# Attention, FFN and gate in one kernel: every third VectorE exp pair as four shifted fp16 terms, made by GpSimd integer adds

## The chip, the cores and the metric

The kernel runs on one core of a Trainium2 chip. A core has TensorE (PE: matmuls, with its weight loads shown as PEld), VectorE (DVE), ScalarE (ACT), GpSimd (POOL) and SyncE (SP, which here only issues DMAs). They run side by side, each through its own queue in order, and wait for each other through semaphores. The metric is the time of one execution on the device in microseconds, where smaller is better. All times here are in microseconds unless marked ns.

## What is computed

A layer norm of `x` (2048 tokens, 512 wide) feeds two branches: attention with 32 query heads of 16 that share one key head and one value head, and a gated FFN of width 1792. The FFN branch, through a silu, gates the attention branch:

```python
xn = layernorm(x)
q = (xn @ wq) as 32 heads of 16;  k = xn @ wk;  v = xn @ wv
p = softmax(q @ k.T * 16 ** -0.5)
s = concat_heads(p @ v) @ wo
g = silu((silu(xn @ w_gate) * (xn @ w_up)) @ w_down)
out = x + s * g
```

The softmax needs 32 x 2048 x 2048 exponentials, 134 million. They are the bulk of the elementwise work.

## The kernel before

**Tiling.** The attention is cut into 32 blocks (`NBLK`): 4 groups of 512 queries, 4 groups of 8 heads, and 2 halves of 4 heads. In a block, each of 16 key tiles of 128 gives two score tiles (`x` is 0 or 1) of 128 keys by 2 heads by 512 queries, 1024 columns of PSUM; 1024 score tiles in all. A score tile is two matmuls (`sc_emit`, line 856) into one of three PSUM slots, `ring[0]` to `ring[2]`. The matmuls p times v of a block accumulate in the PSUM tile `o_ps`; the ones columns in the value weights (`VA`, `VD`) yield the softmax denominator beside it. All scores are scaled so that one unit of exponent of two is 1024.

**Two ways to the exponential.** A tile in `ring[0]` or `ring[1]` goes to ACT (`act_sc`, line 914): one exp of 128x1024 into a buffer `Pb` in bf16 (the first eight tiles of block 1 go into free space, `XB`). Two such tiles give one group of four PE matmuls with the weights `VA`.

A tile in `ring[2]` goes to DVE (`dve_sc`, line 934), two tiles to a pair. "Pass A" (line 942) adds a bias to the score and writes it as uint16 into `Ub`. Read as fp16, those bits are a piecewise linear approximation of two to the power of the score. For the pair's 2048 columns, `dM` (line 955) keeps the mantissa bits and sets an exponent, giving a number between 0.5 and 1; `dE` (line 958) keeps the exponent bits; `dW` (line 960) multiplies the mantissa number by the original. The two results, `Eb` and `Wb`, enter `o_ps` as two terms, weighted by `CE` and `CW` in the two copies of `VD`: a constant plus a quadratic in the mantissa, so that the sum follows the exponential. Each term is one group of four PE matmuls. There are three `Ub` and two each of `Eb` and `Wb`.

**FFN and projections.** Their matmuls are "fill" groups through one PSUM tile, `m_ps`, spread between the score tiles (`g_ffn`, `g_down`, `g_q`, `g_out`). ACT takes a tanh of each, DVE the products. At the end of each pair of blocks the denominators go by DMA through `dn`, a reciprocal, the DRAM scratch `dscr` and a broadcast into `rb`; GpSimd then multiplies `oa` by `rb` into `oT` (line 711). `g_out` multiplies by `wo`, DVE by the gate, and GpSimd adds `x`, which stays in SBUF in `x_sb` (line 675). SP stores the rows.

**What sets the order.** A planner in the kernel, `_Sched`, runs while the program is built. Every operation has an engine, an assumed duration (an ACT exp 0.904, pass A and `dW` 1.135, `dM` and `dE` 0.6, a PE group 0.215), dependencies and a priority. `pe_pick` decides at each step whether PE issues a score tile for ACT, a score tile for DVE, or a ready group; DVE picks pass A before `dM`, `dE` and `dW`. The planned order is then fixed on each engine by `chain`, so each engine's queue runs in exactly that order. When an operation comes later than planned, all that stands behind it on the engine waits. In the prologue `x` is normalised and transposed, 4 rows of 128 tokens at a time; the last four rows of the output have a tail of their own.

Of the kernel before, what the change touches and what calls it, by code (L numbers as in the profile page):

```python
# [1 line left out]

# [8 lines left out]
FP16 = mybir.dt.float16  # L11
# [14 lines left out]
COFF = 4.0  # L26
CE, CW = 0.66858732, 0.66372796 * 1.0
DEN_LO = 16.0
# [5 lines left out]
PB_URG, AHEAD, LAZY, ACTMIN, ACTLOW = 6, 16, 8, 1.7, 1.5  # L34
TOL, MERGE = 0.12, 0.1

# [145 lines left out]
class _Sched:  # L182
    LAT = {"PE": 0.205, "ACT": 0.22, "DVE": 0.25, "POOL": 0.16, "DMA": 0.0, "EXT": 0.0}
    SAME = {"PE": 0.0, "ACT": 0.0, "DVE": 0.1, "POOL": 0.05, "DMA": 0.0}
    SWITCH = 0.105
    HOT = 0.3

    def __init__(self):
        self.free = {"PE": 0.0, "ACT": 0.0, "DVE": 0.0, "POOL": 0.0, "DMA": 0.0}
        self.ready = {e: [] for e in self.free}  # L190
        self.done = []
        self.pe_log = []
        self.seq = 0
        self.mode = None
        self.key = lambda o: o.prio
# [31 lines left out]
    def switch(self, mode):  # L227
        return self.SWITCH if self.mode is not None and mode != self.mode else 0.0

    def pick(self, e):  # L230
        lst = self.ready[e]
        if not lst:
            return None
        if e == "DMA":
            op = min(lst, key=lambda o: (o.ready, o.seq))
            return op.ready, op
        t = self.free[e]
        tm = max(t, min(o.ready for o in lst))
        now = [o for o in lst if o.ready <= tm + 1e-9]
        best = min(now, key=lambda o: (self.key(o), o.seq))  # L240
        if e == "DVE":
            hot = [o for o in lst if o.ready > tm and self.key(o)[0] < 1.6 and self.key(o) < self.key(best)]
            if hot:
                h = min(hot, key=lambda o: (o.ready, o.seq))
                fit = [o for o in now if tm + o.dur <= h.ready + self.HOT]
                best = min(fit, key=lambda o: (self.key(o), o.seq)) if fit else h
        return max(t, best.ready), best

    def place(self, op, start):
        e = op.eng  # L250
        op.start = start
        if e == "PE":
            op.start += self.switch(op.mode)
            self.mode = op.mode
        op.end = op.start + op.dur
        if e != "DMA":
            self.free[e] = op.end
        self.done.append(op)
        if e == "PE":
            self.pe_log.append(op)  # L260
        for u in op.users:
            u.left -= 1
            if u.left == 0:
                self._arm(u)
# [7 lines left out]
def kernel(  # L272
# [79 lines left out]
    vf = sb([P, NT, DH], FP32, "vf")  # L352
    VD = sb([P, 2, NT, 3 * DH], FP16, "VD")
    stats = sb([P, NT, nc.vector.BN_STATS_DIM], FP32, "stats")
    mv = sb([P, NT, nc.vector.BN_AGGR_DIM], FP32, "mv")
# [4 lines left out]
    QB = [sb([P, 512], BF16, f"QB{i}") for i in range(2)]  # L360
    NPB, NU, NE = 8, 3, 2
    Pb = [sb([P, 1024], BF16, f"Pb{i}") for i in range(NPB)]
    XB = [g2_sb[:, 2 * i:2 * i + 2, :].rearrange("p n d -> p (n d)") for i in range(NT // 2)]
    Ub = [sb([P, 2048], U16, f"Ub{i}") for i in range(NU)]
    Eb = [sb([P, 2048], U16, f"Eb{i}") for i in range(NE)]
    Wb = [sb([P, 2048], U16, f"Wb{i}") for i in range(NE)]
    th = [sb([P, 512], FP32, f"th{i}") for i in range(1)] * 2
# [120 lines left out]
    MMF = 0.215  # L488
    NBLK = NSC * NQ * 2
    NTILE = NBLK * NT * 2  # L490
    NPAIR = NSC * NQ
# [14 lines left out]
    def pro_x(c, pr, banks, ev_eng):  # L506
# [3 lines left out]
        for n0 in range(4 * c, 4 * c + 4, step):  # L510
# [22 lines left out]
            for n in range(n0, n0 + step):  # L533
                xo = OP("DVE", 0.33, [r, xr_rel[n % 4]], lambda n=n: e_xn(n), (pr - 0.15 if c == 0 else pr - 0.05, n),
                        name="xn")
                bk = banks[n % 4 // pk]
                h = n % pk
                t_ = OP("PE", 0.26, [xo, brel[bk]] + grp, lambda n=n, bk=bk, h=h: e_tr(n, bank[bk], h), (pr, n), "f",
                        "tr")
                xr_rel[n % 4] = t_  # L540
                grp = grp + [t_]
                if len(grp) == pk:
                    ee = ev_eng if n not in (1, 3) else "DVE"
                    ev = OP(ee, 0.5 if ee == "ACT" else 0.34 if pk == 1 else 0.6, grp,
                            lambda n=n, bk=bk, ee=ee: e_txe(n + 1 - pk, pk, bank[bk], ee), (pr - 0.1, n), name="txe")
                    if c:
                        held.append((grp[0], ev, bk))
                    grp = []
                    brel[bk] = ev
                    evs.append(ev)  # L550
# [24 lines left out]

    held = []
    evs = pro_x(0, 0.3, ("0a", "0b", "1a", "1b"), "ACT")
# [20 lines left out]
    for c in range(1, NSC):  # L598
# [7 lines left out]
        pro_v(c, evs, "2a", 0.7 + 0.01 * c)  # L606
    d_gate = [brel["2a"], brel["2b"], brel["m"]]

    m_rel = [brel["m"]]
# [63 lines left out]
    def e_out_add(n, src, eng):  # L673
        r = res[n % 4]
        return eng.tensor_tensor(out=r[:, :D], in0=src[:, :D], in1=x_sb[:, n, :], op=ALU.add)

# [3 lines left out]
    def g_out(n):  # L680
# [6 lines left out]
        m_rel[0] = m_  # L687
        ad = OP("POOL", 1.3, [m_, xr_rel[n % 4]], lambda: e_out_add(n, ab[i], nc.gpsimd), (0,), name="oadd")
        ab_rel[i] = ad
# [75 lines left out]
    unp = [[[], []] for _ in range(NBLK)]  # L765
    cur = {"ba": 0, "lastx": 1, "nA": 0, "exp": None, "pair": None, "np": 0, "issued": 0, "lastsc": None, "junk": 0, "nX": 0}
    slot = [None, None, None]
    pb_rel, w_rel, e_rel, wop_rel = [], [], [], []
    open_block(0)
# [126 lines left out]

    def act_sc(i, b, x, start):
        sc, t = place_sc(i, b, x, start, MMF)
        cur["lastx"] = x
# [11 lines left out]
        if k >= NPB:  # L911
# [3 lines left out]
                (1,), name="exp")  # L915
        cur["exp"] = ex
        slot[i] = ex
        unp[b][x].append((ex, k, t, buf))
# [16 lines left out]

    def dve_sc(b, x, start, dur):
        sc, t = place_sc(2, b, x, start, dur)
        first = cur["pair"] is None
        u = cur["np"]
        ui = u % NU  # L940
        pa = OP("DVE", 1.135, [sc, wop_rel[u - NU] if u >= NU else None],
                lambda: nc.vector.tensor_scalar(out=Ub[ui][:, x * 1024:(x + 1) * 1024], in0=ring[2][:], scalar1=ubias,  # L942
                                                scalar2=UINF, op0=ALU.add, op1=ALU.min), (1.5, u), name="passA")
        slot[2] = pa
        if first:
            cur["pair"] = (b, x, t, pa)
            return
        _, x0, t0, pa0 = cur["pair"]
        cur["pair"] = None
        cur["np"] += 1  # L950
        pair_blk.append(b)
        half = b % 2
        tx = {x0: t0, x: t}
        ei = u % NE
        o1 = OP("DVE", 0.6, [pa, pa0, w_rel[u - NE] if u >= NE else None], lambda: nc.vector.tensor_scalar(  # L955
            out=Wb[ei][:], in0=Ub[ui][:], scalar1=0x3FF, scalar2=0x3800, op0=ALU.bitwise_and,
            op1=ALU.bitwise_or), (2, u, 0), name="dM")
        o2 = OP("DVE", 0.6, [pa, pa0, e_rel[u - NE] if u >= NE else None], lambda: nc.vector.tensor_scalar(  # L958
            out=Eb[ei][:], in0=Ub[ui][:], scalar1=0x7C00, scalar2=None, op0=ALU.bitwise_and), (2, u, 1), name="dE")
        o3 = OP("DVE", 1.135, [o1, o2], lambda: nc.vector.tensor_tensor(  # L960
            out=Wb[ei][:].bitcast(FP16), in0=Wb[ei][:].bitcast(FP16), in1=Ub[ui][:].bitcast(FP16), op=ALU.mult),
            (2, u, 2), name="dW")
        wop_rel.append(o3)
        for i, (buf, o, rel) in enumerate(((Eb[ei], o2, e_rel), (Wb[ei], o3, w_rel))):
            mms = []
            dps = [o, oev[b - 1]]
            for g in range(4):
                tt = tx[g // 2]
                mms += mm_of(VD[:, i], lambda g, buf=buf: buf[:].bitcast(FP16)[:, g * 512:(g + 1) * 512], tt, half, (g,))
                dps.append(v_ready[tt // 4][i + 1])  # L970
            pv = OP("PE", MMF, dps, pv_emit(b, mms), (1, b, cur["nA"]), "c", "dpv")
            rel.append(pv)
            blk_pv[b].append(pv)
        check_done(b)
# [10 lines left out]
    LB = NBLK - 1  # L985
    LN = 4 * (NSC - 1)

# [99 lines left out]
    def pe_pick():  # L1087
# [42 lines left out]
        if tm is not None:  # L1130
            if ts is None or tm + sd.switch(co.mode) + co.dur <= ts + TOL:
                cands.append(tm)
            else:
                tm = None
        if td is not None and (ts is None or td + sd.switch("r") + MMF <= ts):
            if tm is None or td < tm - 0.2:
# [31 lines left out]
    def pe_do(start, what):  # L1168
# [20 lines left out]
        if kind == "dve":  # L1189
            dve_sc(arg[0], arg[1], start, MMF)  # L1190
            return
# [16 lines left out]
        if dt is not None and tile_ready(*dt) is not None:  # L1208
            at = max(sd.free["PE"], sd.avail(slot[2], "PE"), tile_ready(*dt))
            dve_sc(dt[0], dt[1], at, 0.015 if dt[1] != x else MMF)  # L1210

# [118 lines left out]
```

## Time and profile before

| what | value |
|---|---|
| median of 4 executions (lowest, highest) | 785.98 (784.04, 793.15) |
| the profiled execution | 790.09 |
| its span on the core | 788.3 |
| mean granted PE clock of the span | 0.986 |
| exps on ACT, into `Pb` and into the free space | 770 + 8 |
| pairs on DVE: pass A; `dM`, `dE`, `dW` | 246; 123 each |
| groups on POOL: `oT`; the adds of `x` (both forms) | 15; 14 |
| chain that ended last, by engine | PE 34%, ACT 33%, DVE 20%, issue 9% |

In the profile a group is all instructions of one line, operation and shape. Its busy time is the time in which at least one of them ran; its mean is the length of one. On ACT neighbouring instructions overlap, so that the mean (1167 ns for an exp) is longer than the distance from one to the next. A wait names the instruction that ended it. The chain is followed back from the last instruction to what released each step.

### The profile page before, as it was taken

To read this page: it belongs to the slowest core of one execution; us is meant where nothing else is said; L and a number is where in the kernel's file an instruction comes from. 1 tells how busy PE (TensorE), PEld (TensorE's weight loads), DVE (VectorE), ACT (ScalarE), POOL (GpSimd) and SP (SyncE) were. 2 spreads that over 40 slices of the span, in tenths; PEclk is the share of its full clock that TensorE was granted. 3 is DMA by queue.
4 is the path that set the end of the run, shared out by engine and by line. 5 is a ranking of instruction groups with operands and counts; after the bars stand their busy time and mean duration, and the time that the engine had idled before them with its cause. 6 is when DMAs were issued, how large, how long until landed. Compare 5 with 4: busy or idle time off the path is not lost.

```text
span 788.3 us, 19520 instructions
## 1 busy us (share of the span) xinstructions
PE 726.4 (92%) x8097; PEld 218.8 (28%) x8098; DVE 739.3 (94%) x925; ACT 757.4 (96%) x864; POOL 48.0 (6%) x59
## 2 busy tenths in 40 slices
PE   7999899999999999999989999989999989999994
PEld 3332222222232222222222222222222222222221
DVE  7678999999999999999999989999999989999997
ACT  6899999999999999999999989999999989999993
POOL 2100000000011000001001000000001100000001
PEclk9999999999999999999999889999999989999998
DMA  9300000000010000000000000000001000000001
GB/s 329 114 3 7 17 3 22 2 10 15 5 35 15 23 3 9 16 1 23 3 22 22 16 15 3 22 3 9 16 2 35 16 22 3 3 21 2 23 2 32
DMA packets 19464, 18.50 MB, mean 23 GB/s; under 512 B 8552, under 2 KB 15464, under 8 KB 19368
## 3 DMA queue, kind: packets, MB, share of 16 engines
q1 hardware_dynamic: 17496, 16.37, 6.8%
q8 instruction: 65, 1.06, 0.6%
q10 hardware_dynamic: 1872, 0.82, 0.4%
q14 instruction: 31, 0.25, 0.1%
HBM read 12.62 MB, written 2.34 MB: 19 GB/s over the span
## 4 chain that ended last, share of the span: by engine, by line
PE 34%; ACT 33%; DVE 20%; issue 9%; DMA 1%; SPq 1%; POOL 0%; ACTq 0%; DVEq 0%
ACT Pb L914 28%; PE ring L856 14%; PE m_ps L474 12%; PE o_ps L726 7%; DVE Ub L942 7%; DVE Wb L960 4%; ACT th L637 3%; DVE Eb L958 2%; DVE Wb L955 2%; ACT th L654 1%; SPq L753 1%; DMA dn<-oa 1%; DVE ab L639 1%; DVE hT L643 1%; DVE oa L739 1%
## 5 line engine op out<-in xcount | busy, mean ns | idle before, releaser
L914 ACT ACTIVATE Pb<-ring 128x1024 bf16<-128x1024 f32 x770 | 728.7, 1167 | 11.2 <-PE ring L856 10.9
L856 PE MATMUL ring<-QB,KT 32*128 32x512 bf16 x2048 | 320.8, 383 | 40.9 <-ACT Pb L914 32.8
L942 DVE TENSOR_SCALAR Ub<-ring 128x1024 uint16<-128x1024 f32 x246 | 299.3, 1216 | 13.4 <-PE ring L856 8.5
L856 PEld LDWEIGHTS <-KT 32*128 32x128 bf16 x2048 | 106.1, 91 | 350.1 <-issue 345.6
L960 DVE TENSOR_TENSOR Wb<-Wb,Ub 128x2048 f16<-128x2048 f16 x123 | 150.4, 1223 | 0.0
L726 PE MATMUL o_ps<-Pb,VA 128*32 128x512 bf16 x1540 | 149.7, 389 | 0.4 <-DVE oa L739 0.4
L955 DVE TENSOR_SCALAR Wb<-Ub 128x2048 uint16<-128x2048 uint16 x123 | 86.9, 708 | 0.1
L958 DVE TENSOR_SCALAR Eb<-Ub 128x2048 uint16<-128x2048 uint16 x123 | 86.1, 705 | 0.0
L474 PE MATMUL m_ps<-xnT,wg_sb 128*32 128x512 bf16 x896 | 74.0, 384 | 0.5 <-DVE g_sb L656 0.3
L474 PE MATMUL m_ps<-xnT,wu_sb 128*32 128x512 bf16 x896 | 71.6, 392 | 1.3 <-DVE ab L639 1.2
L474 PE MATMUL m_ps<-wd_sb,hT 128*32 128x512 bf16 x896 | 71.9, 383 | 0.0
L711 POOL TENSOR_TENSOR oT<-oa,rb 128x512 bf16<-128x512 f32 x15 | 20.7, 1379 | 608.8 <-DMA rb<-dscr 560.8
L726 PEld LDWEIGHTS <-VA 128*32 128x32 bf16 x1556 | 38.7, 94 | 54.8 <-issue 54.1
L726 PE MATMUL o_ps<-Eb,VD 128*32 128x512 f16 x492 | 48.7, 390 | 2.1 <-DVE Eb L958 1.8
L726 PE MATMUL o_ps<-Wb,VD 128*32 128x512 f16 x492 | 49.1, 389 | 1.4 <-DVE Wb L960 0.9
L637 ACT ACTIVATE th<-m_ps 128x512 f32<-128x512 f32 x56 | 41.9, 749 | 0.0
L726 PEld LDWEIGHTS <-VD 128*32 128x32 f16 x984 | 29.4, 94 | 43.1 <-issue 41.0
L643 DVE TENSOR_TENSOR hT<-ab,m_ps 128x512 bf16<-128x512 f32 x56 | 38.1, 680 | 2.7 <-PE m_ps L474 2.4
L639 DVE SCALAR_TENSOR_TENSOR ab<-th,m_ps 128x512 f32<-128x512 f32 x56 | 38.0, 678 | 1.6 <-ACT th L637 1.0
L474 PEld LDWEIGHTS <-wg_sb 128*32 128x32 bf16 x896 | 17.3, 94 | 27.3 <-issue 26.5
L474 PEld LDWEIGHTS <-wu_sb 128*32 128x32 bf16 x896 | 16.6, 95 | 27.1 <-issue 24.9
L739 DVE COPY oa<-o_ps 128x512 f32<-128x512 f32 (+1 forms) x33 | 22.0, 668 | 1.5 <-PE o_ps L726 1.5
(106 smaller groups left out, 246.2 us busy)
## 6 DMA issues: line engine op xcount, KB each, us to landing
rb<-dscr SPq DMA_DIRECT2D x15, 256.0 KB
dn<-oa SPq DMA_DIRECT2D x120, 2.0 KB, 1.7
oa<-oa SPq DMA_DIRECT2D x60, 32.0 KB, 2.0
wg_sb<-in_B_w_gate_dram SPq DMA_DIRECT2D x1, 1792.0 KB, 12.0
wu_sb<-in_B_w_up_dram SPq DMA_DIRECT2D x1, 1792.0 KB
wd_sb<-in_B_w_down_dram SPq DMA_DIRECT2D x1, 1792.0 KB, 19.8
out_dram<-xn SPq DMA_DIRECT2D x14, 128.0 KB, 2.0
x_sb<-in_A_x_dram SPq DMA_DIRECT2D x3, 512.0 KB
```

The costliest lines, as they stand in the source:

```text
L474: return [nc.tensor.matmul(out=dst[GRP * j:GRP * j + GRP, :], lhsT=w[:, GRP * j:GRP * j + GRP], rhs=rhs, start=start, stop=stop, tile_posi ...
L637: t_ = OP("ACT", 0.477, [a], lambda: nc.scalar.activation(out=th[i][:], in_=m_ps[:], func=ACT.Tanh, scale=0.5), (0,), name="tanh")
L639: s_ = OP("DVE", 0.6, [t_, ab_rel[i]], lambda: nc.vector.scalar_tensor_tensor(out=ab[i][:], in0=th[i][:], scalar=1.0, in1=m_ps[:], op0=ALU ...
L643: h = OP("DVE", 0.6, [b], lambda: nc.vector.tensor_tensor(out=hT[:, f, :], in0=ab[i][:], in1=m_ps[:], op=ALU.mult), (1,), name="hmul")
L726: r.append(nc.tensor.matmul(out=o_ps[GRP * g:GRP * g + GRP, :], lhsT=lhs, rhs=rhs, start=(n == 0), stop=(n == pv_total[(b, g)] - 1), tile_ ...
L739: oev[b] = sd.new(_Op("DVE", 0.6, [], lambda: [nc.vector.tensor_copy(out=oat[:, a:z], in_=o_ps[:, a:z]) for a, z in cuts], (0.2,), name="o ...
L856: return lambda: [nc.tensor.matmul(out=ring[sl][:, u * 512:(u + 1) * 512], lhsT=KT[half][GRP * g:GRP * g + GRP, t * P:(t + 1) * P], rhs=QB ...
L914: lambda: nc.scalar.activation(out=buf, in_=ring[i][:], func=ACT.Exp, scale=escale, bias=ebias),
L942: lambda: nc.vector.tensor_scalar(out=Ub[ui][:, x * 1024:(x + 1) * 1024], in0=ring[2][:], scalar1=ubias, scalar2=UINF, op0=ALU.add, op1=AL ...
L955: o1 = OP("DVE", 0.6, [pa, pa0, w_rel[u - NE] if u >= NE else None], lambda: nc.vector.tensor_scalar(out=Wb[ei][:], in0=Ub[ui][:], scalar1 ...
L958: o2 = OP("DVE", 0.6, [pa, pa0, e_rel[u - NE] if u >= NE else None], lambda: nc.vector.tensor_scalar(out=Eb[ei][:], in0=Ub[ui][:], scalar1 ...
L960: o3 = OP("DVE", 1.135, [o1, o2], lambda: nc.vector.tensor_tensor(out=Wb[ei][:].bitcast(FP16), in0=Wb[ei][:].bitcast(FP16), in1=Ub[ui][:]. ...
```

## The change

`dve_sc` gets a second form. Where the pair's number is a multiple of `KE` = 3, GpSimd's planned backlog is under `KB` = 3 and the weights are built, the pair has no `dM`, `dE` and `dW`. Pass A uses another bias, and GpSimd makes three further copies of its result, each by adding 256, 512 or 768 to every 16-bit number. Two numbers lie in one 32-bit integer, so the constant is 65537 times the offset (`koff`), and one add covers 512 integers; there are six adds of 128x512 to a pair, three behind each pass A. Read as fp16 the four copies are the piecewise linear function, shifted by quarters of an octave. Their weighted sum follows the exponential; the weights are `VD[:, 0]` for the first and `VK[0]` to `VK[2]` for the others. A pair so has four PE groups in place of two.

The buffers `Ub`, `Eb` and `Wb` become one pool of nine, `Bf`: seven tiles and two in `x_sb`'s first eight rows, once these have been normalised. `VK[1]` and `VK[2]` lie in its third group of four rows. The add of `x` at the output therefore loads its rows again by DMA, except for the last four, which stay.

The planner gets a lock: GpSimd's operations and DVE's `dM`, `dE`, `dW` and `xn` are planned so that none of one engine overlaps one of the other. `pe_pick` issues a DVE tile first when DVE's planned backlog is short, and its tolerances change (`TOL` from 0.12 to 0.17; `DPRI`, `DTOL`, `DWIN` are new). In the code the new adds are named `kadd`.

```diff
+K4 = (0.24037645, 0.20213265, 0.16996992, 0.14292964)
+KOFF = 256.0
+DPRI, DTOL, DWIN = 1.2, 0.12, 0.15
-TOL, MERGE = 0.12, 0.1
+TOL, MERGE, KE, KB = 0.17, 0.1, 3, 3.0
...
+    def rdy(self, o):
+        if o.eng == "DVE" and o.name in self.LOCKS:
+            return max(o.ready, self.lock["POOL"])
+        if o.eng == "POOL":
+            return max(o.ready, self.lock["DVE"])
+        return o.ready
...
-    Ub = [sb([P, 2048], U16, f"Ub{i}") for i in range(NU)]
-    Eb = [sb([P, 2048], U16, f"Eb{i}") for i in range(NE)]
-    Wb = [sb([P, 2048], U16, f"Wb{i}") for i in range(NE)]
+    Bf = [sb([P, 2048], U16, f"Bf{i}")[:] for i in range(7)]
+    Bf += [x_sb[:, 4 * c:4 * c + 4, :].rearrange("p n d -> p (n d)").bitcast(U16) for c in range(2)]
...
+    def vk_build(i):
+        v = VK[i].rearrange("p t (w d) -> p t w d", d=DH)
+        src = vf[:].rearrange("p t (o d) -> p t o d", o=1).to_broadcast([P, NT, 2, DH])
+        w = CE * 2.0 ** (-(i + 1) / 4)
+        return [nc.gpsimd.memset(v[:, :, 1:2, :], w),
+                nc.gpsimd.tensor_scalar(out=v[:, :, 0:3:2, :], in0=src, scalar1=w, scalar2=0.0, op0=ALU.mult, op1=ALU.add)]
...
-        ad = OP("POOL", 1.3, [m_, xr_rel[n % 4]], lambda: e_out_add(n, ab[i], nc.gpsimd), (0,), name="oadd")
+        ld = OP("DMA", 2.2, [xr_rel[n % 4]], lambda: nc.sync.dma_start(out=res[n % 4][:, :D], in_=x_v[:, n, :]), (0,))
+        ad = OP("POOL", 1.3, [m_, ld], lambda: e_out_add(n, ab[i], nc.gpsimd), (0,), name="oadd")
...
+    kbias = ubias - 1024.0 * math.log2(CE / K4[0])
...
+    def k4_ok():
+        pend = sum(o.dur for o in sd.ready["POOL"]) + cur.get("kpend", 0.0)
+        pend = sum(o.dur for o in k_ops if o.start is None)
+        return cur["np"] % KE == 0 and planned(vk_ready) and max(sd.free["POOL"] - sd.free["PE"], 0.0) + pend < KB
...
+        kadd = []
+        if k4:
+            for i in range(3):
+                bi, brl = kb[i]
+                kadd.append(OP("POOL", 1.0, [pa] + brl, lambda i=i, bi=bi: nc.gpsimd.tensor_tensor(
+                    out=Bf[bi][:, hs].bitcast(I32), in0=U[:, hs].bitcast(I32),
+                    in1=koff[:, i:i + 1].to_broadcast([P, 512]), op=ALU.add),
+                    (2, u), name="kadd"))
+            k_ops.extend(kadd)
...
+        if k4:
+            cur["nk"] = cur.get("nk", 0) + 1
+            terms.append((ui, [pa, pa0], VD[:, 0], None, 1))
+            for i in range(3):
+                terms.append((kb[i][0], [kadd[i], kadd0[i]], VK[i], [vk_ready[i]], 0))
+        else:
+            (wi, wrel), (ei, erel) = get_buf(), get_buf()
...
-        if td is not None and (ts is None or td + sd.switch("r") + MMF <= ts):
+        if td is not None and (ts is None or td + sd.switch("r") + MMF <= ts + DTOL):
+            back = max(sd.free["DVE"] - F, 0.0) + sum(o.dur for o in sd.ready["DVE"])
+            if back < DPRI and td <= F + DWIN:
+                return td, ("dve", dt)
```

## The prediction

> **What bounds the kernel now.** I read the busy line of the page first, then a table of stretches, then the groups of ScalarE (ACT) and VectorE (DVE), then the waits of the steady part, 70 to 770 us.
>
> ```profile
> PE 726.4 (92%) x8097; PEld 218.8 (28%) x8098; DVE 739.3 (94%) x925; ACT 757.4 (96%) x864; POOL 48.0 (6%) x59
> ```
>
> Three engines are over 90% and GpSimd (POOL) is nearly empty. The stretch table (length; busy PE, PEld, DVE, ACT, POOL; granted PE clock) settles which one binds:
>
> ```profile
> 120.00:220.00 100.00, 94.44 (x1066) 28.37 (x1059) 97.62 (x115) 100.00 (x115) 2.54 (x2) 1.00 0.05 12
> ...
> 450.00:460.00 10.00, 10.00 (x76) 1.67 (x72) 6.81 (x9) 7.00 (x8) 0.49 (x1) 0.54 0.15 43
> ```
>
> ACT is busy without a gap; DVE has 2.4% to spare. In the second line the PE clock fell to 0.54 and ACT lost 3.0 us: PE is the engine that can starve ACT. The waits (who, for whom: us in total, times, longest):
>
> ```profile
> PE ring L856 <- ACT Pb L914: 30.6, 78, 1.0
> DVE Ub L942 <- PE ring L856: 8.5, 20, 2.4
> ACT Pb L914 <- PE ring L856: 6.8, 14, 1.4
> ...
> PE ring L856 <- DVE Ub L942: 3.4, 9, 0.9
> ```
>
> PE waits for ACT, not the reverse. ACT's price per tile is its pitch, not the 1167 ns that its group shows, since one exp starts before the last has ended:
>
> ```profile
> 299.30 8.52 ACT L914 ACTIVATE Pb<-ring 128x1024 bf16<-128x1024 f32 x9
> ```
>
> Nine exps in 8.52 us, the last lasting 1.167, give (8.52 - 1.17) / 8 = **0.919 us**. On DVE the pitches from the timeline are 1.13 (pass A, 363.31 to 364.44), 0.60 (a mask operation, 509.85 to 510.45) and 1.14 (the product, 303.26 to 304.40).
>
> **What the skill says.** (1) The Trainium skill, "SBUF — State Buffer", Who interferes with whom: GpSimd and VectorE share a port pair as an exclusive lock; a VectorE operation in a two-port mode, or one with two SBUF inputs against a GpSimd operation that reads SBUF, blocks the other for its whole length, while one with a single input outside those modes does not. The trace agrees in both directions. POOL, then DVE (start, length):
>
> ```profile
> 410.96 1.28 POOL L711 TENSOR_TENSOR oT<-oa,rb 128x512 bf16<-128x512 f32 x1 [44.18 <-DMA rb<-dscr]
> ...
> 411.14 1.65 DVE L958 TENSOR_SCALAR Eb<-Ub 128x2048 uint16<-128x2048 uint16 x1
> ```
>
> ```profile
> 364.44 1.21 DVE L960 TENSOR_TENSOR Wb<-Wb,Ub 128x2048 f16<-128x2048 f16 x1
> ...
> 364.46 2.33 POOL L711 TENSOR_TENSOR oT<-oa,rb 128x512 bf16<-128x512 f32 x1 [43.83 <-DMA rb<-dscr]
> ```
>
> A mask that takes 0.684 us (median) took 1.65 because GpSimd held the port until 412.24; GpSimd's 1.27 became 2.33 behind a product. Pass A reads PSUM: at 744.22 an oT ran 1.28, unstretched, beside a pass A that lasted until 744.56. (2) "VectorE: DVE Perf Modes", the perf-mode tier table: 693 ns for a 2048-element 16-bit tensor_scalar, 1224 for tensor_tensor; the trace has 0.684 and 1.215, so masks are two-port operations and the product has two SBUF inputs. Both kinds lock. (3) "GPSIMD Engine Reference", Elementwise: a two-input add of 2048 fp32 takes 4497 ns; a quarter is an estimate of 1.12 us for 512. The trace has 1.15 to 1.27 for such adds and products.
>
> **The change part by part.** The built program's order shows 128 VectorE pairs for 123, and 42 of them in the new form (252 GpSimd adds, 6 a pair), so 86 keep masks and product.
>
> *ACT*: 10 exps fewer (770 to 760; the 8 into g_sb stay): 10 x 0.919 = **-9.2 us**. This is the only thing taken from the binding engine.
>
> *DVE*: 37 pairs' worth of masks and product go, 37 x (0.60 + 0.60 + 1.14) = -86.6; 10 pass A come, 10 x 1.13 = +11.3; so 739 falls to 664 before port waits. None of it is gain by itself, since DVE wasn't the bound.
>
> *POOL*: 252 adds with a stride-0 second operand, an operation not in the trace. Lower bound 0.61 (the one-input copy of 128x512 into wk_rep), upper 1.27 (oT); I take 1.15, the two-input row with one bf16 input: 290 us, 37% of the span. Beside it three builds of VK, about 0.9 us each (a memset at 0.3, a 512-element operation at 0.6), after the last VD build at 45.9, where POOL next has work at 83.6: nothing.
>
> *The port*: 290 + 48 for POOL and 86 x 2.34 = 201 for DVE's locking operations make 539 of some 780 us, so both fit. Unordered, an operation of DVE would meet a running add in 37% of cases and wait half of it: 258 x 0.37 x 0.58 = 55 us on DVE, 719 in all, still under today's 739. In the order only 56 of the 258 stand directly behind an add, so the planner has spaced many.
>
> *PE*: 94 groups of four more for the terms (246 to 340), 5 fewer for Pb, 3 fewer zero fillers: 86 x 0.22 (eight matmuls in 0.62 against four in 0.40) = +18.9, and 13 fewer changes of array shape at 0.10 = -1.3: +17.6 us. Its cover is the 30.6 us that PE waits for ACT; if that is gone, the cost shows as PE's 34% share of the chain, 6 us.
>
> *Waits on POOL*: the four term products wait for adds. Laid along ACT's queue, an add stands a median of 5.5 us ahead of the PE group that reads it, only 8 of 252 under 1.4. Adds can also queue behind oT, which waits for the rb broadcast: before, oT came 13.2 and 11.6 us after the second o_ps copy ended (306.1 to 319.36, 543.6 to 555.16); in the new order it stands 7.4 to 18.9 us behind it. Most adds behind it have room; I take **+1 us**, bounds 0 and 5. The shared buffers make pass A and masks wait on adds, none nearer than 1.8 us: 0.
>
> *SP*: 12 loads of x rows, 128 KB each, about 0.64 us of SP each (the rb issue) and landing like out_dram's 2.0. SP waits 473.7 us for oa copies, and the loads need only an old buffer: 0. If each delayed the dn chain in front of oT, 12 x 0.64 = 8 us; I keep that for the range.
>
> *Port leak*: what of DVE's blocking reaches ACT through PE, which issues scores in order, isn't in the trace. Below nothing it can't be; unordered, see the first rival. I take **+2 us**, some six late operations at 0.33.
>
> Sum against the profiled execution (790.09; span 788.3 and 1.8 around it): 790.1 - 9.2 + 1 + 2 = 783.9. That execution stands 4.1 above the median of 785.98, so the forecast is **780**.
>
> **Rivals.** *The port makes DVE late (slower).* A late pass A or product holds PE's in-order queue, and the score of ACT's next tile stands behind. The distance from pass A to the next score of that slot is a median of 1.84 us in both orders, near what pass A and its semaphores need; with a slack of about 0.25, my choice, each of 258 x 0.37 = 95 meetings passes on 0.33: +31, so 786 - 9 + 31 = **808**. It decides once 28 meetings pass that much on. For it: DVE's blocked rows above, and adds in runs of three. Against: the order spaces them, DVE has 75 us more idle before port waits, and at 781.3 a DVE add got the port between two back-to-back POOL adds (the second took 1.59 for 1.15), so it isn't starved through a run. *PE becomes co-bound*: its 17.6 us fall where no ACT wait covers them, or draw another clock dip at 3 us: 786 - 9 + 6 to 10 = **783 to 787**. For it: PE's 34% of the chain. Against: PE's 30.6 us of waits. *The integer add is slow*: above (780 - 249) / 252 = 2.1 us the port itself is full; at 2.3 (twice my value) it needs 829 us, so about **830**. No row speaks for it; nothing excludes it. *Few pairs qualify*: excluded by the 252 adds in the order.
>
> **How the numbers follow.** Under 1% a measurement of this kernel can't be told from no change, so the limits are 778.1 and 793.8. ACT-bound with a small leak 0.60, its own range 774 to 787, its centre close to the limit: half faster, half the same. PE co-bound 0.13, nearly all the same. Port 0.21 and slow add 0.06, nearly all slower. Together faster 0.34, same 0.40, slower 0.26. The range 771 to 805 leaves out the slow add and the upper half of the port case.
>
> **What would show it.** ACT 760 exps at the same pitch, still near 100% in the steady stretches; DVE near 665 to 720 busy with masks of 1.2 to 1.8 us among those of 0.68; POOL near 340 with adds of 1.15; PE's wait for ACT down to about 13 us. Wrong if ACT's steady stretches show gaps of several per cent ending on PE's scores, PE's waits on DVE rise from 6 us to tens, or adds last over 1.5 us unblocked.

## The result and the profile after

The changed kernel takes 791.42 us (median of 42 runs) against 788.0 (63 runs of the kernel before); the measured ratio is **1.0052, interval 1.0039 to 1.0064** (the bare quotient of the medians is 1.0043). It is slower by some half a per cent, where the forecast was a gain of 0.8%. The profiled execution has a span of 788.8 us against 788.3, so the two traces show how a gain and a loss of the same size cancel.

Most of the spread between executions of one kernel goes with the granted PE clock. Over the 71 executions of the kernel before that were taken with the experiments, in three sets, the time falls by 5.2 to 6.3 us for each 0.01 of mean clock, with correlations of -0.94 to -0.97. The two profiled executions, at 0.987 and 0.986, are a fair pair. The medians are 3.4 us apart; the changed kernel's executions have a median clock of 0.986 and those 71 one of 0.991, which by these slopes is an estimate of 2.6 to 3.2 us.

The busy line of the page after:

```profile
PE 731.7 (93%) x8442; PEld 216.1 (27%) x8443; DVE 696.4 (88%) x827; ACT 750.4 (95%) x854; POOL 356.3 (45%) x317
```

ScalarE lost 7 us of busy time and VectorE 43, and the span didn't follow. The chain that ended last, by engine:

```profile
PE 43%; ACT 28%; DVE 15%; issue 8%; DMA 3%; POOL 1%; SPq 1%; ACTq 0%; DVEq 0%; POOLq 0%
```

PE went from 34% to 43%, ScalarE from 33% to 28%. The rows of the groups (columns as before: busy time and mean ns of one, then the idle time before them) name the exps (8 of the 768 stand in a row of their own, with another output buffer), the new adds and the old form's products:

```profile
L954 ACT ACTIVATE Pb<-ring 128x1024 bf16<-128x1024 f32 x760 | 716.3, 1109 | 14.1 <-PE ring L894 11.7
...
L1021 POOL TENSOR_TENSOR Bf<-Bf,koff 128x512 int32<-128x512 int32 x182 | 220.4, 1232 | 246.1 <-DVE Bf L1013 206.5
...
L1048 DVE TENSOR_TENSOR Bf<-Bf,Bf 128x2048 f16<-128x2048 f16 x41 | 54.5, 1330 | 0.0
```

In these rows an add lasts 1.232 in the mean and a product 1.330, both above the undisturbed lengths given below. The table of stretches (columns as before) shows that ScalarE isn't without gaps any more:

```profile
120.00:220.00 100.00, 96.04 (x1130) 27.56 (x1127) 93.93 (x100) 98.91 (x112) 47.18 (x38) 1.00 0.05 13
220.00:320.00 100.00, 92.00 (x1072) 26.40 (x1068) 91.28 (x100) 97.88 (x112) 51.77 (x43) 1.00 0.08 22
```

And the waits from 70 to 770 us:

```profile
DVE Bf L1013 <- PE ring L894: 24.1, 43, 1.8
...
PE ring L894 <- ACT Pb L954: 19.6, 50, 1.0
...
ACT Pb L954 <- PE ring L894: 10.2, 20, 1.5
...
PE o_ps L763 <- POOL Bf L1021: 2.9, 2, 1.5
```

VectorE now waits for PE (8.5 us before, 24.1 in the first of its two rows now), and ScalarE waits for PE half as much again as before (6.8). PE waits twice for an add, and no wait of VectorE is put down to GpSimd.

**A measure that the busy share hides.** A recorded exp lasts some 1.1 us, but in both traces the most common distance from one start to the next is 0.904 us: the records overlap. The last of the nine exps from which the prediction takes its pitch, and the tanh behind it, stand so in the trace of before:

```profile
306.53 1.28 ACT L914 ACTIVATE Pb<-ring 128x1024 bf16<-128x1024 f32 x1
307.44 0.87 ACT L637 ACTIVATE th<-m_ps 128x512 f32<-128x512 f32 x1
```

An exp that starts 0.2 us late still touches the end of the one before, and ScalarE looks 100% busy. I therefore count *gaps*: the time from the start of the first exp to the end of the last, less 0.904 for each exp and 0.48 for each of the 72 tanhs (307.44 to 307.92 in the trace of before). By this count ScalarE had 24.0 us of gaps before the change, so it was never without slack. The 72 tanhs are taken off even where some stand behind the last exp (one in the changed kernel, e7 and e10, four in e3 and e5, three in e4); there the true gaps are 0.5 to 1.9 larger. The balance of the two spans, in us:

| | before | after | difference |
|---|---|---|---|
| exps x 0.904 | 778: 703.3 | 768: 694.3 | -9.0 |
| gaps between first and last exp | 24.0 | 28.7 | +4.7 |
| from the end of the last exp to the end | 13.6 | 18.3 | +4.7 |
| the rest (start, tanhs) | 47.4 | 47.5 | +0.1 |
| span | 788.3 | 788.8 | +0.5 |

The tail is read directly from the timelines. After, on PE and then ScalarE:

```profile
769.09 0.61 PE L763 MATMUL o_ps<-Pb,VA 128*32 128x512 bf16 x8
...
769.53 1.25 PE L493 MATMUL m_ps<-wd_sb,hT 128*32 128x512 bf16 x20
...
770.83 0.60 PE L493 MATMUL m_ps<-wd_sb,hT 128*32 128x512 bf16 x8
...
771.49 0.60 ACT L690 ACTIVATE th<-m_ps 128x512 f32<-128x512 f32 x1 [0.99 <-PE m_ps L493]
...
772.86 0.66 PE L1079 MATMUL m_ps<-ident_f,oa 128*128 128x128 f32 x4 [0.35 <-DVE g_sb L692]
```

Before:

```profile
762.68 0.61 PE L474 MATMUL m_ps<-wd_sb,hT 128*32 128x512 bf16 x8
...
765.92 0.44 PE L990 MATMUL m_ps<-ident_f,oa 128*128 128x128 f32 x2
```

Before, the last FFN matmuls (`wd_sb`) were done at 763.3, over 11 us ahead of the end of the last exp at 774.7. After, 28 of them run behind the last scores, the exps end at 770.5, and the tanh and the transposes that follow have nothing left to hide behind. In the order of the changed kernel 11 fill groups stand behind the last score, the 7 groups of these 28 matmuls and the 4 transposes at 772.86; before, none did.

Where the gaps come from shows on VectorE and GpSimd (start, length):

```profile
317.80 1.95 DVE L1048 TENSOR_TENSOR Bf<-Bf,x_sb 128x2048 f16<-128x2048 f16 x1
```

```profile
317.63 3.02 POOL L1021 TENSOR_TENSOR Bf<-Bf,koff 128x512 int32<-128x512 int32 x2
```

A product that takes 1.215 started during an add and took 1.95; the second add then waited for it, and two adds took 3.02 in place of 2.07 (the median add lasts 1.037). Over the run the 258 masks and products are 32.6 us longer than their undisturbed medians, against 6.4 for 369 of them before.

The trace also shows what the adds leave alone. Of the changed kernel's 256 pass A, 101 ran at least nine tenths of their length beside a GpSimd operation, and their median is 1.218 us, as it is for the 125 that met none; the exps agree too (1.122 and 1.121). The 33 masks that ran so have a median of 1.082 against 0.683, the 16 products 1.44 against 1.214.

### The profile page after: what moved, and what is told of

The parts are those of the page before. It is cut to its first block, busy times and chain, and to the rows that moved or that the text cites. A ratio compares the mean times of both kernels' runs of the same rounds, so it can differ in the third digit from the quotient of the medians.

```text
span 788.8 us, 20413 instructions
## 1 busy us (share of the span) xinstructions
PE 731.7 (93%) x8442; PEld 216.1 (27%) x8443; DVE 696.4 (88%) x827; ACT 750.4 (95%) x854; POOL 356.3 (45%) x317
## 4 chain that ended last, share of the span: by engine, by line
PE 43%; ACT 28%; DVE 15%; issue 8%; DMA 3%; POOL 1%; SPq 1%; ACTq 0%; DVEq 0%; POOLq 0%
ACT Pb L954 24%; PE ring L894 16%; PE m_ps L493 15%; PE o_ps L763 11%; DVE Bf L1013 3%; ACT th L673 3%; DVE x_sb L1013 2%; DVE Bf L1046 2%; DVE Bf L1048 2%; DVE Bf L1043 1%; DMA rb<-dscr 1%; DVE ab L675 1%; POOL Bf L1021 1%; ACT th L690 1%; SPq L790 1%
## 5 line engine op out<-in xcount | busy, mean ns | idle before, releaser
L954 ACT ACTIVATE Pb<-ring 128x1024 bf16<-128x1024 f32 x760 | 716.3, 1109 | 14.1 <-PE ring L894 11.7
L1021 POOL TENSOR_TENSOR Bf<-Bf,koff 128x512 int32<-128x512 int32 x182 | 220.4, 1232 | 246.1 <-DVE Bf L1013 206.5
L1013 DVE TENSOR_SCALAR Bf<-ring 128x1024 uint16<-128x1024 f32 x208 | 253.3, 1218 | 30.3 <-PE ring L894 25.8
L894 PEld LDWEIGHTS <-KT 32*128 32x128 bf16 x2048 | 91.9, 91 | 334.0 <-issue 329.6
L1021 POOL TENSOR_TENSOR x_sb<-Bf,koff 128x512 int32<-128x512 int32 x40 | 50.2, 1258 | 44.1 <-DVE Bf L1013 34.3
L763 PE MATMUL o_ps<-Bf,VD 128*32 128x512 f16 x652 | 64.0, 390 | 4.7 <-DVE Bf L1046 2.1
L1013 DVE TENSOR_SCALAR x_sb<-ring 128x1024 uint16<-128x1024 f32 x48 | 58.5, 1218 | 6.8 <-PE ring L894 5.0
L1048 DVE TENSOR_TENSOR Bf<-Bf,Bf 128x2048 f16<-128x2048 f16 x41 | 54.5, 1330 | 0.0
L1021 POOL TENSOR_TENSOR Bf<-x_sb,koff 128x512 int32<-128x512 int32 x28 | 34.6, 1259 | 27.1 <-DVE x_sb L1013 24.7
L1046 DVE TENSOR_SCALAR Bf<-Bf 128x2048 uint16<-128x2048 uint16 x53 | 40.4, 762 | 0.0
L1043 DVE TENSOR_SCALAR Bf<-Bf 128x2048 uint16<-128x2048 uint16 x41 | 35.0, 853 | 0.2
L1048 DVE TENSOR_TENSOR x_sb<-x_sb,Bf 128x2048 f16<-128x2048 f16 x26 | 34.4, 1322 | 0.0
## 6 DMA issues: line engine op xcount, KB each, us to landing
wg_sb<-in_B_w_gate_dram SPq DMA_DIRECT2D x1, 1792.0 KB, 11.5
```

Source lines behind the costliest of these rows:

```text
L763: r.append(nc.tensor.matmul(out=o_ps[GRP * g:GRP * g + GRP, :], lhsT=lhs, rhs=rhs, start=(n == 0), stop=(n == pv_total[(b, g)] - 1), tile_ ...
L894: return lambda: [nc.tensor.matmul(out=ring[sl][:, u * 512:(u + 1) * 512], lhsT=KT[half][GRP * g:GRP * g + GRP, t * P:(t + 1) * P], rhs=QB ...
L954: lambda: nc.scalar.activation(out=buf, in_=ring[i][:], func=ACT.Exp, scale=escale, bias=ebias),
L1013: lambda: nc.vector.tensor_scalar(out=U[:, hs], in0=ring[si][:], scalar1=bias, scalar2=UINF, op0=ALU.add, op1=ALU.min), (1.5, u), name="pa ...
L1021: kadd.append(OP("POOL", 1.0, [pa] + brl, lambda i=i, bi=bi: nc.gpsimd.tensor_tensor(out=Bf[bi][:, hs].bitcast(I32), in0=U[:, hs].bitcast( ...
L1043: o1 = OP("DVE", 0.6, [pa, pa0] + wrel, lambda: nc.vector.tensor_scalar(out=Bf[wi], in0=U, scalar1=0x3FF, scalar2=0x3800, op0=ALU.bitwise_and,
```

## The experiments

The theories: **PE** (the new form's 86 more groups fill PE, so scores come later and other work is left for the end), **port** (adds block VectorE's masks and products, and what waits for these), **wait** (PE stands behind late adds) and **planner** (the new picking rule costs the time). Gaps, tail and lengthening are each of one profiled execution; the groups behind the last score are of the built order. The ratio is the measured one, with its interval; it isn't the bare quotient of the two medians, from which it stands up to 0.4%, so sizes in us are given both ways where it matters.

| kernel | ratio (interval) | exps | gaps | tail | fill groups behind last score | lengthening of masks and products |
|---|---|---|---|---|---|---|
| before | 1 | 778 | 24.0 | 13.6 | 0 | 6.4 |
| after | 1.0052 (1.0039, 1.0064) | 768 | 28.7 | 18.3 | 11 | 32.6 |
| e1 new form off | 1.0015 (0.9990, 1.0039) | 780 | 21.5 | 13.2 | 0 | 7.2 |
| e2 two of four groups | 0.9945 (0.9917, 0.9972) | 766 | 37.1 | 13.2 | 0 | 32.2 |
| e3 no adds, own plan | 0.9832 (0.9793, 0.9871) | 754 | 12.1 | 33.6 | 54 | 5.0 |
| e4 before + PE groups | 1.0110 (1.0070, 1.0151) | 778 | 21.9 | 27.9 | 34 | 8.8 |
| e5 old picking rule | 1.0186 (1.0123, 1.0249) | 772 | 23.0 | 32.5 | 51 | 26.1 |
| e7 no adds, same plan | 0.9829 (0.9768, 0.9890) | 768 | 17.1 | 18.2 | 11 | 5.5 |
| e8 TOL 0.20 | 0.9990 (0.9959, 1.0021) | 766 | 29.3 | 13.1 | 0 | 29.9 |
| e9 every sixth pair | 0.9998 (0.9960, 1.0037) | 774 | 26.0 | 14.0 | 0 | 22.6 |
| e10 adds nobody reads | 1.0049 (1.0018, 1.0079) | 768 | 28.9 | 17.3 | 11 | 36.5 |
| e11 before + adds | 1.1059 (1.0972, 1.1145) | 778 | 103.0 | 13.8 | 0 | 65.6 |
| e12 two terms | 0.9858 (0.9799, 0.9917) | 754 | 31.1 | 13.1 | 0 | 12.8 |
| e13 two terms, every second | 0.9707 (0.9657, 0.9757) | 746 | 27.0 | 13.2 | 0 | 8.3 |

**e1, the new form off.** All else of the change stays.

```diff
-        return cur["np"] % KE == 0 and planned(vk_ready) and max(sd.free["POOL"] - sd.free["PE"], 0.0) + pend < KB
+        return False and planned(vk_ready) and max(sd.free["POOL"] - sd.free["PE"], 0.0) + pend < KB
```

> The changed kernel with the new form of a pair switched off; the shared buffers, the loads of x rows, the VK builds, the lock and the new picking rule of the planner stay. 780 exps on ScalarE, 122 old pairs, no GpSimd adds. PE theory (the 86 added PE groups of the new form fill PE, so that scores come later and FFN work is left over at the end): back to the kernel before, ratio 0.998 to 1.004. Port theory (adds block VectorE): the same, as there are no adds. Planner theory (the new picking rule and tolerances open gaps on ScalarE): stays at the changed kernel's 1.005 or above.

1.0015, an interval that holds 1. Shared buffers, x loads, lock and picking rule together cost nothing that shows while no pair has the new form: the loss needs the new form. The planner theory, which asked for 1.005, falls.

**e2, two of the four PE groups.** The other two terms are left out of the computation; the adds stay.

```diff
-            for i in range(3):
-                terms.append((kb[i][0], [kadd[i], kadd0[i]], VK[i], [vk_ready[i]], 0))
+            terms.append((kb[0][0], [kadd[0], kadd0[0]], VK[0], [vk_ready[0]], 0))
+            for i in (1, 2):
+                buf_rel[kb[i][0]] = [kadd[i], kadd0[i]]
```

> The changed kernel, but a pair of the new form uses only two of its four terms in PE groups, as an old pair does (the other two terms are left out of the computation); all six GpSimd adds are still made. 766 exps. PE theory: with PE relieved the saved exps show, 12 x 0.904 = 11 us less than before: ratio 0.985 to 0.991, the last FFN work done before the last exp. Port theory: the adds still block VectorE, 1.003 to 1.007. Planner theory: 1.003 to 1.007.

0.9945, between the two: 1.1% below the changed kernel (0.7% by the medians), so PE's groups count, but short of the 0.985 to 0.991 that PE alone would give. The tail is back at 13.2. Something else, still there with the adds, takes 0.4 to 1%. (Its profiled execution has a mean PE clock of 0.975, so its 37.1 of gaps is above what the median run can have.)

**e3, no adds, planned anew.** Every term reads pass A's own result; the shifts are left out of the computation.

```diff
-            kb = [get_buf() for _ in range(3)] if k4 else []
+            kb = [(ui, None)] * 3 if k4 else []
...
-            for i in range(3):
+            for i in range(0):
...
-                terms.append((kb[i][0], [kadd[i], kadd0[i]], VK[i], [vk_ready[i]], 0))
+                terms.append((ui, [pa, pa0], VK[i], [vk_ready[i]], 0))
...
```

> The changed kernel without the GpSimd adds: all four PE groups of a new pair read pass A's own result (the shifts are left out of the computation). With no lock to plan around, the planner gives VectorE 135 pairs and ScalarE 754 exps; PE has some 100 groups more than the kernel before. Port theory: 24 exps fewer are worth 22 us: ratio 0.970 to 0.978. PE theory: PE is as full or fuller than in the changed kernel, so nearly all of it is lost again: 0.995 to 1.008. Planner theory: 0.975 to 0.985.

0.9832, again between port and PE. It lies in the planner theory's range too, but e1 speaks against that theory. The gaps fall to 12.1 (14.1 with the late tanhs) though PE has more matmuls than in the changed kernel (8471 for 8442), which fits adds that make gaps; the tail grows to 33.6 with 54 groups left over, so PE's surplus goes to the tail. The plan is another one here, so e7 has to show the part of the adds.

**e4, PE's groups alone.** The kernel before with two groups of zero weights behind every third pair.

```diff
+        if u % 3 == 0:
+            for o in (o1, o2):
+                blk_pv[b].append(OP("PE", MMF, [o, oev[b - 1]], pv_emit(b, [(zw[:], xnT[:, 0, 0:512], g) for g in range(4)]),
+                                    (1, b, cur["nA"]), "c", "dpv"))
```

> The kernel before, with two more PE groups of zero weights behind every third pair (82 groups of four matmuls, 18 us of PE by the pitch of 0.22), nothing else changed on purpose. PE theory: the time rises by 9 to 14 us, ratio 1.011 to 1.018, with FFN work or later scores at the end. Port and planner theory: PE's waits for ScalarE of 30 us hide it, 1.000 to 1.004.

1.0110, just inside what PE forecast (1.0150 by the medians). The last exp ends no later than before (772.5) and the gaps are no larger; all of the cost stands behind it, as PE's timeline shows:

```profile
774.30 3.19 PE L474 MATMUL m_ps<-wd_sb,hT 128*32 128x512 bf16 x56
778.92 3.21 PE L474 MATMUL m_ps<-wd_sb,hT 128*32 128x512 bf16 x56 [1.42 <-DVE g_sb L656]
```

Two runs of 14 FFN groups, 3.2 us each, stand where ScalarE has no exp left. The planner puts such work between two scores only where it fits (`TOL`), and 82 more groups took the places. At this tolerance PE's 30.6 us of waiting for ScalarE were no cover; they lie in pieces (78 waits, the longest 1.0 us).

**e5, the picking rule of before on the new form.**

```diff
-DPRI, DTOL, DWIN = 1.2, 0.12, 0.15
-TOL, MERGE, KE, KB = 0.17, 0.1, 3, 3.0
+DPRI, DTOL, DWIN = -1.0, 0.0, 0.15
+TOL, MERGE, KE, KB = 0.12, 0.1, 3, 3.0
```

> The changed kernel with the picking rule of the kernel before (TOL 0.12, no head start for VectorE tiles): 772 exps, 41 new pairs. In its order 51 of the 784 FFN and projection groups still stand behind the last score, against 11 in the changed kernel and none in the kernel before. PE theory: the stretch behind the last exp grows from 18 to 28 to 34 us, fewer gaps before it, ratio 1.006 to 1.018. Planner theory (the new rule costs the time): faster than the changed kernel, 0.993 to 1.001.

1.0186, just above PE's range, and a tail of 32.5, inside it. The new picking rule is what keeps the tail at 18. The larger tolerance and the head start went together here; e8 speaks for the tolerance.

**e7, the same plan without the adds.** From pair 15 on the planned adds aren't emitted (228 of 252; the shifted copies are left out of the computation).

```diff
-                kadd.append(OP("POOL", 1.0, [pa] + brl, lambda i=i, bi=bi: nc.gpsimd.tensor_tensor(
+                kadd.append(OP("POOL", 1.0, [pa] + brl, lambda i=i, bi=bi: [] if u >= 15 else nc.gpsimd.tensor_tensor(
```

> The changed kernel in exactly its own order on PE, ScalarE and VectorE, but from pair 15 on GpSimd's adds are not made (the shifted copies are left out of the computation; PE reads what the buffers hold). 228 of 252 adds go and nothing else. Port theory: 32 us of blocked VectorE operations and the waits behind them go, ratio 0.990 to 0.996. PE theory: PE's groups are the same, so it stays at 1.002 to 1.006. The stretch behind the last exp stays at 18 us in both.

0.9829, lower than any theory had it. With PE, ScalarE and VectorE in exactly the order of the changed kernel, 17 us go by the ratios (0.9829 / 1.0052) and 14.6 by the medians (776.80 against 791.42); in the profiled executions 11.5, from 788.8 to 777.3, all of it in the gaps, while the tail stays at 18.2. The smallest figure is the one at a like clock. e7's four executions had clocks of 0.990 to 0.997 and the slowest of them, at 0.990, took 779.12; six executions of the changed kernel at 0.989 took 788.0 to 791.4. ScalarE's wait for PE:

```profile
ACT Pb L954 <- PE ring L894: 2.4, 5, 0.7
```

10.2 us before the adds went, 2.4 now. So the adds cost more than the whole gain of the exps. Whether by the port or by PE's waits for them, this run doesn't tell.

**e10, the adds made, but for nobody.**

```diff
+    dump = [g2_sb[:, 2 * i:2 * i + 2, :].rearrange("p n d -> p (n d)").bitcast(I32) for i in (6, 7)]
...
-                    out=Bf[bi][:, hs].bitcast(I32), in0=U[:, hs].bitcast(I32),
+                    out=(dump[i % 2] if 15 <= u < 108 else Bf[bi][:, hs].bitcast(I32)), in0=U[:, hs].bitcast(I32),
```

> The changed kernel in its own order, but in pairs 15 to 107 GpSimd's adds (186 of 252) write into a tile that nothing else reads; PE reads what the term buffers hold (the shifted copies are left out of the computation there). The adds and their hold on the port stay, the waits of PE for them go. Port theory (blocked VectorE operations cost the 17 us that the missing adds gave back): stays at 0.999 to 1.006. Wait theory (PE stands behind late adds): falls to 0.983 to 0.990.

1.0049: the whole cost is back, with 36.5 us of lengthened masks and products, though no matmul waits for any of these adds. The waits from 70 to 770 us:

```profile
ACT Pb L955 <- PE ring L895: 10.9, 18, 1.6
...
PE o_ps L764 <- POOL Bf L1022: 1.8, 1, 1.8
```

The one wait for an add is for one of the 66 that are still read. No wait of VectorE is put down to GpSimd, in e7 or here, so buffers that the adds hold aren't the cost either, and the two profiled executions had nearly the same clock (0.990 and 0.989). With e7 this settles it for the port; the wait theory falls.

**e11, the adds alone, unplanned.** The kernel before with 198 adds that nothing reads.

```diff
...
+        if u % 3 == 0 and 6 <= u < 105:
+            for i in range(3):
+                OP("POOL", 1.0, [pa], lambda i=i: nc.gpsimd.tensor_tensor(
+                    out=dump[i % 2], in0=Ub[ui][:, x * 1024:(x + 1) * 1024].bitcast(I32),
+                    in1=koff[:, i:i + 1].to_broadcast([P, 512]), op=ALU.add), (2, u), name="kadd")
```

> The kernel before, its orders on PE, ScalarE and VectorE unchanged, with three GpSimd adds behind each pass A of every third pair from 6 to 104 (198 adds) into a tile that nothing reads; nothing is planned around them. Port theory: the adds meet masks and products and cost 10 to 25 us, ratio 1.012 to 1.030, with VectorE's masks lengthened by some 30 us in sum. Wait theory: nothing waits for these adds, 1.000 to 1.004.

1.1059: the direction was right and the size wrong, 83 us for a forecast of 10 to 25. The lengthening, 65.6 us, is about double the forecast 30, and ScalarE's gaps grow by 79.0, more than the lengthening does. VectorE had 94% to do, which left little room for a delay. The waits, from 70 to 770 us:

```profile
ACT Pb L918 <- PE ring L860: 71.3, 103, 2.6
...
PE o_ps L730 <- DVE Eb L967: 20.0, 26, 2.0
```

The chain runs as the port rival had it: VectorE late, PE behind it (58.0 us of waits for VectorE in all, 8.8 before), ScalarE behind PE. The mean PE clock also fell, to 0.925; what that added wasn't separated. By the slopes above, carried far beyond the clocks that gave them, it is an estimate of 34 to 42 us against the 0.991 of the kernel before, so up to half of the 83. That 252 adds cost the changed kernel 11 to 17 us and 198 cost this one 83 fits the planner's lock and the relief of VectorE; no run takes these two apart.

**e8 and e9, more room for PE and fewer pairs.** e8 is the changed kernel with `TOL` 0.20; e9 has also `KE` 6. The first added line is e8's, the second e9's.

```diff
-TOL, MERGE, KE, KB = 0.17, 0.1, 3, 3.0
+TOL, MERGE, KE, KB = 0.2, 0.1, 3, 3.0
+TOL, MERGE, KE, KB = 0.2, 0.1, 6, 3.0
```

> The changed kernel with TOL 0.20 for 0.17, so that a group may push ScalarE's next score a little further back: 766 exps, 42 new pairs, and no FFN group behind the last score. PE theory, left-over work: the stretch behind the last exp falls from 18 to 13 to 14 us, ratio 0.997 to 1.003; if PE is simply full, the gaps between exps grow by what the tail loses, 1.003 to 1.007. Port theory: 1.003 to 1.007.

> The changed kernel with every sixth pair in the new form (KE 6) and TOL 0.20: 20 new pairs with 120 adds, 774 exps, 44 more groups for VectorE's terms than the kernel before in place of 94, no FFN group behind the last score. PE theory: 4 exps fewer are worth 3.6 us and PE's extra work is half: ratio 0.994 to 1.000. Port theory: half the adds, half the loss, 1.000 to 1.004.

0.9990 and 0.9998, both intervals holding 1. e8 brings the tail back to 13.1, as PE forecast, and leaves the gaps at 29.3: the tail part of the loss was left-over work, and a wider tolerance found places for it. Whether it paid for them in the gaps is less sure: this profiled execution, at a clock of 0.997, is 4 us under e8's own median. By the ratios e8 is 4.9 us below the changed kernel, where the shorter tail and two exps fewer would give 7.0. Neither run beats the kernel before; the lengthening stays at 29.9 in e8 and 22.6 in e9. e9's 0.9998 fits the end of what PE expected and the start of what port expected, and tells nothing apart.

**e12 and e13, a form with two terms.** Two costs point to a pair with fewer adds and fewer groups: pass A's result and one copy, half an octave further. The weights are set so that the mean error is nothing (0.48045 and 0.48045 divided by the root of 2). An error of at most 1.0% then stands in a single exponential, by the formula, where four terms have 0.2%. e12 is this edit alone; e13 has also `KE` 2 and `TOL` 0.24 in place of 3 and 0.17.

```diff
-K4 = (0.24037645, 0.20213265, 0.16996992, 0.14292964)
+K4 = (0.48045301, 0.33973158)
...
-            kb = [get_buf() for _ in range(3)] if k4 else []
+            kb = [get_buf()] if k4 else []
...
-            for i in range(3):
-                bi, brl = kb[i]
+            for i in (1,):
+                bi, brl = kb[0]
...
-            for i in range(3):
-                terms.append((kb[i][0], [kadd[i], kadd0[i]], VK[i], [vk_ready[i]], 0))
+            terms.append((kb[0][0], [kadd[0], kadd0[0]], VK[1], [vk_ready[1]], 0))
```

> The changed kernel with a new pair of two terms in place of four: pass A's own result and one copy shifted by half an octave, weights 0.48045 and 0.33973. Two adds and two PE groups a pair; 754 exps, 88 adds, 12 PE groups more than the kernel before in sum, no FFN group behind the last score. PE and port together: 24 exps fewer are worth 22 us, of which a third of the adds takes 4 to 6 and the groups 1: ratio 0.977 to 0.984. If the shared buffers or the planner's rule were the cost: 0.990 or above.

> The same two-term form for every second pair, TOL 0.24: 746 exps, 138 adds, 70 old pairs. 32 exps fewer are worth 29 us, the adds take 6 to 9, PE's fuller queue 3 to 6: ratio 0.974 to 0.984. If PE bounds it (it has no room left beside ScalarE's scores): 0.985 to 0.995, with gaps between exps above those of the form for every third pair.

0.9858 and **0.9707**: e12 lies just above what was expected (its four executions had a mean PE clock of 0.970 to 0.982), e13 below. e13, at 764.0 us against 787.55, beats both kernels. The page's busy line of e13:

```profile
PE 704.9 (92%) x8138; PEld 206.3 (27%) x8139; DVE 661.2 (87%) x801; ACT 728.4 (96%) x832; POOL 243.7 (32%) x203
```

32 exps fewer than before are 28.9 us at 0.904; its span, 762.2, is 26.1 below before's. The tail is 13.2; the gaps, at 27.0, are 3 above before's. Every second pair in the new form leaves 70 old pairs, so 210 masks and products meet 138 adds, and their lengthening is down to 8.3.

## Why the prediction was wrong

- **ScalarE, -9.2**: right in kind. Ten exps fewer are 9.0 us at a distance of 0.904. The pitch of 0.919 is a slip in the reading: it takes the group's mean of 1.167 for the length of the last of the nine exps, which is 1.28 as shown above, and (8.52 - 1.28) / 8 is 0.905.
- **"ACT is busy without a gap"**: wrong. The busy share covers gaps under some 0.2 us; by the count of starts there were 24 us of gaps, 1.6 of them in the stretch shown as 100.00. It still was the engine with the largest busy share.
- **The port leak, "+2 us, some six late operations at 0.33"**: the term that failed first. By e7 and e10 it is 11.5 us in the profiled executions, and 14 to 17 between medians or ratios, where the clock differs too. The meetings were fewer than the unordered count (59 of 258 lengthened by more than 0.1 us, for 95), and their sum, 26 us above before's, was half the 55 reckoned for the worst. But far more than 2 us passes on: e7 takes 27.1 us of lengthening away (32.6 to 5.5), and 11.5 of time go with it. The port rival had, with 31 us, too high a price; its point of decision, 28 meetings at 0.33 or 9 us, was passed. Its chain shows only in part: the sign that was named, PE's waits for VectorE in the tens, came in e11 alone. In the changed kernel they are 12.5 us (8.8 before, 9.2 in e7), while ScalarE's waits for PE are 11.5 against 3.3 in e7. How each late operation reaches ScalarE wasn't followed.
- **PE, "its cover is the 30.6 us that PE waits for ACT"**: failed too, at the planner's tolerance of 0.17. PE waited in 78 pieces of at most 1.0 us. The surplus pushed FFN work out of the places between scores, to the end: +4.7 in the tail. e4 prices 82 groups at 8.7 us by the ratio and 11.8 by the medians, for 18 us of PE work. With a tolerance of 0.20 in e8 the left-over work is gone, so it was the planner's rule together with the surplus that left it, not the pieces alone. The text looked for PE's loss in ScalarE's gaps or in a clock dip; that an order can shift it to the end wasn't asked, though the built order has the 11 groups behind the last score.
- **VectorE, "none of it is gain by itself"**: not confirmed. Without the adds, at the same order, the gaps are 17.1 against 24.0 before. Some 7.0 of before's lie in the two stretches of low clock (at 450 and 640 us), which is as much as the difference, so whether VectorE's relief gave anything stays open.
- **POOL, 1.15 an add**: the add takes 1.037 undisturbed and 1.237 in the mean with the port's waits. The waits for adds at PE and behind oT were priced at +1; the trace has two at PE, 2.9 us in all, and e10, without them, isn't faster by more than the noise.
- **The lock of POOL and VectorE** (the Trainium skill, "SBUF — State Buffer", Who interferes with whom): confirmed in both directions, with a size. No mask or product of the changed kernel was lengthened by more than 1.12 us, about one add: a waiting VectorE operation gets the port after the add in progress, not after the run of three.

In sum -9.0 by the exps, +4.7 in the gaps (a port loss of 11.5, less the 6.9 by which e7's gaps lie below before's), +4.7 in the tail. The likeliest case was right about the size of ScalarE's gain, and wrong that two costs were covered. These +0.5 are of two executions at a like clock; the medians are 3.4 us apart, and by the estimate above most of the rest goes with the lower clock of the changed kernel's executions. Why that clock is lower wasn't tried. The forecast of 780 also started from 785.98, a median of four; over 63 executions it is 788.0.

## What to carry to other kernels

Work that is moved to an idle engine isn't free where it holds a port of a busy one: price it by the operations it lengthens, and ask what stands behind these in queues of fixed order. Idle time in many pieces covers whole groups only as far as the order's own rule lets them in: look in the built order for the work that is pushed out, and where it ends up, which may be behind the last instruction of the bounding engine. And read that engine's saturation from the distances between starts, not from a busy share of overlapping records.

## What the runs showed of the hardware that wasn't expected

A 32-bit integer add of 128x512 with a stride-0 second operand took 1.037 us on GpSimd, less than the two-input operations with fp32 in the trace (1.15 to 1.27). It lengthened VectorE's masks and products, and neither pass A, which reads PSUM, nor ScalarE's exps. Unplanned, 198 such adds (205 us of GpSimd at that length) slowed a kernel with VectorE at 94% by 10.6%, though nothing read their results; planned around the lock, 252 of them cost 1.5 to 2.2%. In the unplanned run the mean granted PE clock was 0.925, against 0.986 before, with PE idle more often (89% busy for 92%); what lowers it wasn't tried, and part of the 10.6% may be its doing.
